# Token tiles of 504 and 496 columns in place of 512 and 384

## The chip, the cores and the metric

The kernel runs on one core of one Trainium2 chip. The metric is the device time of one execution in microseconds. Engines are named as the profile names them: PE is TensorE's matmul, PEld its weight load, DVE is VectorE, ACT is ScalarE, POOL is GpSimd, SP is SyncE, whose queue issues nearly all DMAs.

## The reference, cut to what matters

```python
def _attn_ref(q, k, v, tau):                 # B, N, C = 2, 6016, 256
    qn = q / (np.linalg.norm(q, axis=1, keepdims=True) + 1e-06)
    kn = k / (np.linalg.norm(k, axis=1, keepdims=True) + 1e-06)
    s = kn.transpose(0, 2, 1) @ qn / tau     # 256 x 256 for each batch
    a = softmax(s)
    return v @ a                             # 6016 tokens x 256

def _moe_ref(x, w_gate, w_val, w_out):       # d_ff 1536
    gate = 1.0 / (1.0 + np.exp(-(x @ w_gate)))
    return gate * (x @ w_val) @ w_out

def _moe2_ref(x, w_in, w_out):               # d_ff 2048
    h = x @ w_in
    return (h - np.tanh(h)) @ w_out

x = attn(q, k, v, tau).reshape(12032, 256)
out = _moe2_ref(_moe_ref(x))
```

The attention is over channels: scores are 256 x 256 for each batch, and the softmaxed matrix multiplies every token of the batch. What follows works on each token by itself. So 12032 tokens, 6016 in each of two batches, run through four products, and how they are cut into tiles is free, but that a tile may not reach over the end of a batch.

## The kernel before

The kernel holds tokens as columns. A tile is a range of at most 512 tokens of one batch, since 512 float32 numbers fill one bank of PSUM. `token_tiles` (lines 57 to 66) makes the list: eleven tiles of 512 and one of 384 in the first batch, and the same turned round in the second, so that the two tiles of 384 are neighbours, the 12th and the 13th of 24.

Before the tiles run, about the first 57 us, the scores of the first batch are summed over 47 groups of 128 token rows (`qk_scores`, L278), normalized and softmaxed, and the attention matrix is multiplied into the gate and value weights (`aw_block`). With that the value product of the attention disappears as a step of its own: stage 1 multiplies the raw v by those combined weights.

Data for the matmuls are split into a high and a low part of type float32r, so each product takes three matmuls: weight high by data high, weight low by data high (`prod_h`, L475 and L476), weight high by data low (`prod_l`, L480). For each tile i:

- Stage 1, 12 units c: `s1_mm` makes the gate and value products of 128 hidden channels each, two PSUM tiles `ps` with six matmuls each. ACT takes the sigmoid (L515), DVE multiplies (L516). `part_b` splits the result (L580 on ACT, L581 on DVE or GpSimd), and `part_c` adds it into two accumulators `y` (six matmuls).
- Stage 2, 16 units m: `s2_mm` makes `h` (six matmuls), `s2_a` works out h - tanh(h) on ACT and DVE (L539 to L560), `part_b` splits, `part_c` adds into two accumulators `o` (six matmuls). After the last unit they are copied out and sent (L642, L643).

So a tile takes 12 x 12 + 12 x 6 + 16 x 6 + 16 x 6 = 408 matmuls, each over all columns of the tile. The order of the work is written out: a list of units is sorted by a position that goes by the unit's number alone, not by its columns, and stage 2 of a tile runs between the units of stage 1 of the next. Each unit's three parts follow each other with a lag of three units. In between, from the third tile on, a list of side steps makes the scores of the second batch (matmuls of 256 columns, L283 to L285) and then its combined weights.

PSUM has eight banks. Four of them are a ring, from which `ps`, `h` and the side steps' tiles are taken. A new tile in the ring waits, on TensorE, until the last reader of the tile that had its bank is done. The program hands out the banks when it is built, and not strictly in turn.

v is loaded a tile ahead (`load_v`, L339): the load for tile i + 1 is issued when tile i has been split. The very last unit works on two halves of its tile (`HALVES`, L585, and `finish`), so that the two halves overlap on the way out.

Of the kernel before, what the change touches and what calls it, by code (L numbers as in the profile page):

```python
# [18 lines left out]
B, S, D = 2, 6016, 256  # L19
# [4 lines left out]
TPB = 12  # L24
CH = 512
NM = 512
NW = 12
NO = 6
NI = 8
# [27 lines left out]
def token_tiles():  # L57
    out = []
    for b in range(B):
        off = 0  # L60
        sizes = [NM] * (S // NM) + [S % NM]
        for n in sizes if b < B - 1 else sizes[::-1]:
            out.append((b, off, b * S + off, n))
            off += n
        assert off == S
    return out
# [3 lines left out]
def attn_moe_kernel(  # L70
# [125 lines left out]
    wo_t = [base.tile([P, 2, CH], F32R, name=f"wo{c}") for c in range(NO)]  # L196
    wgv_d = dram.tile([NW // 2, P, 2, 2, CH], F32, name="wgv_d")


    wgv_t = [wp.tile([P, 2, 2, CH], F32R, name=f"wgv{f}") for f in range(NW // 2)]  # L200

    def wgv_item(f, jc):
        return (wgv[2 * f + jc], lambda: wgv_t[f][:, :, jc, :], f"wgv{f}_{jc}")

    def wo_item(c):
        return (wo[c], lambda: wo_t[c], f"wo{c}")

    conv0 = [wgv_item(0, jc) for jc in range(2)]
    conv = [wgv_item(1, jc) for jc in range(2)]
    for f in range(2, NW // 2):  # L210
        conv += [wgv_item(f, 0), wgv_item(f, 1), wo_item(f - 2)]
# [107 lines left out]
    def aw_block(aT, rs, wt, ic, dst, name):  # L319
# [8 lines left out]
        nc.vector.scalar_tensor_tensor(dst[:, 1, ic, :], ps, rs[:, ic : ic + 1], dst[:, 0, ic, :].bitcast(F32), op0=ALU.mult, op1=ALU.subtract)  # L328

    tiles = token_tiles()  # L330
    NT = len(tiles)
    raws, vhl = {}, {}

    def load_v(i):
        if i >= NT:
            return
        b, off, _, n = tiles[i]
        t = vp.tile([P, 2, NM], F32, tag="vraw", name=f"vraw{i}")
        nc.sync.dma_start(t[:, :, :n], vT[b].rearrange("(c p) n -> p c n", p=P)[:, :, off : off + n])  # L339
        raws[i] = t  # L340

    def split_v(i, between=lambda: None, eng=nc.vector):
        n = tiles[i][3]
        t = raws.pop(i)
        vhl[i] = [vp.tile([P, 2, NM], F32R, tag=f"vhl{ic}", name=f"vhl{i}_{ic}") for ic in range(2)]
        for ic in range(2):
# [61 lines left out]
    for t in (1, 0):  # L408
        for c in range(2):
            o = 2 * (2 * t + c)  # L410
# [37 lines left out]
    def new_aw(f, b):  # L448
        return ap_.tile([P, 2, 2, CH], F32R, tag=f"aw{f}", name=f"aw{f}_{b}")

    aws = {0: [new_aw(f, 0) for f in range(NW // 2)], 1: []}
    mp = ctx.enter_context(tc.tile_pool(name="mp", bufs=1, reuse_waits="tile"))
    aT0 = mp.tile([P, 2, 2, D], F32R, name="aT0", tag="yhl")
    for ic in range(2):
        cs = slice(ic * P, (ic + 1) * P)
# [17 lines left out]
    def prod_h(ps, n, wts, xs, first, skip=False):  # L473
        for j, ((wh, wl), (xh, _)) in enumerate(zip(wts, xs)):
            mm(ps[:, :n], wh, xh, start=first and j == 0, stop=False, skip_group_check=skip)  # L475
            mm(ps[:, :n], wl, xh, start=False, stop=False, skip_group_check=skip)  # L476

    def prod_l(ps, n, wts, xs, last, skip=False):
        for j, ((wh, _), (_, xl)) in enumerate(zip(wts, xs)):
            mm(ps[:, :n], wh, xl, start=False, stop=last and j == len(wts) - 1, skip_group_check=skip)  # L480
# [30 lines left out]
    def s1_act(i, c):  # L511
        n = tiles[i][3]
        G, V = live[1, i, c]
        sg = mp.tile([P, NM], F32, tag="sg", bufs=2, name=f"sg{i}_{c}")
        nc.scalar.activation(sg[:, :n], G[:, :n], AF.Sigmoid)  # L515
# [13 lines left out]
    def late(i, m):  # L529
        return i == NT - 2 and m >= LATE or i == NT - 1 and m < K2 - 1  # L530

    def s2_a(i, m, mid):
        n = tiles[i][3]
        H = live[2, i, m][:, :n]
        u = m2.tile([P, NM], F32, tag="u", bufs=2, name=f"u{i}_{m}")[:, :n]
        d = m2.tile([P, NM], F32, tag="d", bufs=2, name=f"d{i}_{m}")[:, :n]
        s = (yp if m % 2 and (i == NT - 1 or late(i, m)) else m2).tile([P, NM], F32, tag="s", bufs=2, name=f"s{i}_{m}")[:, :n]
# [11 lines left out]
        else:  # L549
# [5 lines left out]
            else:  # L555
                mid()
                nc.scalar.activation(big, u, AF.Relu, bias=c_m[:, 0:1])
            for cs in HALVES if (2, i, m) == LAST else (slice(0, n),):
                nc.vector.scalar_tensor_tensor(s[:, cs], s[:, cs], C_D, w[:, cs], op0=ALU.add, op1=ALU.mult)
# [13 lines left out]
    def part_b(u):  # L573
# [4 lines left out]
        eng = nc.gpsimd if kind == 2 and (late(i, c) or u[1:] == LAST or c < 2 * i < 6) else nc.vector  # L578
        for cs in HALVES if u[1:] == LAST else (slice(0, n),):
            nc.scalar.copy(hl[:, 0, cs], x[:, cs])  # L580
            (nc.vector if cs == HALVES[1] else eng).tensor_sub(hl[:, 1, cs], x[:, cs], hl[:, 0, cs].bitcast(F32))  # L581
        live[kind, i, c] = hl

    LAST = (2, NT - 1, K2 - 1)
    HALVES = [slice(h * NM // 2, (h + 1) * NM // 2) for h in range(2)]  # L585

    def finish(hl, ws, pos):

        acc = ops[NT - 1]

        def high(o, h):
            prod_h(acc[o][:, HALVES[h]], NM // 2, [ws[o]], [(hl[:, 0, HALVES[h]], None)], False, True)

        def low(o, h):
            prod_l(acc[o][:, HALVES[h]], NM // 2, [ws[o]], [(None, hl[:, 1, HALVES[h]])], True, True)

        def put(o):
            for h, cs in enumerate(HALVES if o else [slice(0, NM)]):
                t = m2.tile([P, NM], F32, tag=("out", "d")[h], bufs=2, name=f"out{NT - 1}_{o}_{h}")
                (nc.scalar.copy if o else nc.vector.tensor_copy)(t[:, cs], acc[o][:, cs])  # L600
                (nc.scalar if h else nc.sync).dma_start(outT[o * P : (o + 1) * P, pos + cs.start : pos + cs.stop], t[:, cs])

        high(0, 0)
        high(1, 0)
        high(0, 1)
        low(0, 0)
        low(0, 1)
        put(0)
        high(1, 1)
        low(1, 0)  # L610
        low(1, 1)
        put(1)
# [122 lines left out]
    def wblock(f):  # L735
        if f < NW // 2:
            t = qp.tile([P, 2, 2, CH], F32R, tag="wb", name=f"wb{f}")
            nc.sync.dma_start(t.bitcast(F32), wgv_d[f])
            q1["wb", f] = t

    def side_aw(f, ic):
# [4 lines left out]
        if ic == 1:  # L746
            wblock(f + 1)
            if f + 1 == NW // 2:
                q2ctx.close()
# [164 lines left out]
```

## Time and profile before

| what | value |
|---|---|
| time, median of 3 runs | 2304.48 us (2304.45 to 2304.77) |
| the profiled execution | 2304.04 us |
| its span, first to last instruction | 2302.2 us |
| PE busy | 2296.7 us, 10434 matmuls recorded |
| PEld busy | 1928.0 us |
| DVE busy | 1815.5 us |
| ACT busy | 1582.1 us |
| POOL busy | 83.1 us |
| mean granted clock of TensorE | 0.999 of 2.4 GHz |
| DMA | 83.08 MB, mean 36 GB/s |

The span is what the profile sees; the 1.8 us between it and the execution's time lie before its first and after its last instruction. An engine's busy time says in how much of the span it had something under way. For a pipelined engine like TensorE that can be all of the span although it works below its pace; its pace is read from the starts of its instructions.

### The profile page before, as it was taken

What the parts mean: (1) busy time and instruction counts of PE and PEld (TensorE: products, weight loads), DVE (VectorE), ACT (ScalarE), POOL (GpSimd) and SP (SyncE); (2) the same over time, 40 slices, a digit from 0 to 9 for tenths busy, and PEclk for the clock granted to TensorE, in tenths of its full rate; (3) what the DMA queues carried; (4) which work ended last, traced back from release to release, by engine and by line L of the source; (5) the groups of instructions that cost most, each with busy time, mean ns of one, the idle gap of its engine ahead of it and who ended that gap; (6) DMA issues with size and microseconds to landing.
All of it is one profiled execution on the core that took longest, in us unless ns stands there. A gap on an engine that the chain in (4) does not pass through costs nothing.

```text
span 2302.2 us, 28360 instructions
## 1 busy us (share of the span) xinstructions
PE 2296.7 (100%) x10434; PEld 1928.0 (84%) x10434; DVE 1815.5 (79%) x2891; ACT 1582.1 (69%) x2884; POOL 83.1 (4%) x64
## 2 busy tenths in 40 slices
PE   9999999999999999999999999999999999999999
PEld 8888888888888888888899988888888888888887
DVE  6878879888888888877777777777777777786778
ACT  7657777676776677766666666666666667666668
POOL 5000000000000000000000000000000000000007
PEclk9999999999999999999999999999999999999999
DMA  8630001110101101001110000000000000000000
GB/s 333 248 114 1 24 23 33 33 37 19 37 28 33 37 23 37 4 32 35 55 37 17 6 11 19 1 19 10 10 19 2 18 19 1 19 10 10 10 1 19
DMA packets 39786, 83.08 MB, mean 36 GB/s; under 512 B 4192, under 2 KB 18272, under 8 KB 38112
## 3 DMA queue, kind: packets, MB, share of 16 engines
q1 hardware_dynamic: 39216, 80.89, 10.4%
q8 instruction: 81, 1.33, 0.2%
q14 instruction: 57, 0.47, 0.1%
q10 hardware_dynamic: 432, 0.39, 0.1%
HBM read 62.39 MB, written 18.87 MB: 35 GB/s over the span
## 4 chain that ended last, share of the span: by engine, by line
PE 99%; ACT 0%; DMA 0%; issue 0%; POOL 0%; SPq 0%
PE ps L476 11%; PE ps L475 11%; PE ps L480 11%; PE o L480 7%; PE h L476 7%; PE h L480 7%; PE h L475 7%; PE o L475 7%; PE o L476 7%; PE y L480 6%; PE y L476 6%; PE y L475 6%; PE S0o L278 1%; PE S0y L278 1%; PE aw L326 0%; PE aw L325 0%
## 5 line engine op out<-in xcount | busy, mean ns | idle before, releaser
L476 PE MATMUL ps<-vhl,aw 128*128 128x512 f32 (+1 forms) x1152 | 443.6, 385 | 0.0
L475 PE MATMUL ps<-vhl,aw 128*128 128x512 f32 (+1 forms) x1152 | 443.5, 385 | 0.0
L544 DVE TENSOR_TENSOR d<-h,d 128x512 f32<-128x512 f32 (+1 forms) x366 | 247.8, 677 | 237.1 <-ACT d L540 237.0
L580 ACT CAST hl<-s 128x512 fp32r<-128x512 f32 (+1 forms) x385 | 235.2, 611 | 274.8 <-DVE s L548 271.9
L539 ACT ACTIVATE u<-h 128x512 f32<-128x512 f32 (+1 forms) x384 | 226.7, 590 | 242.5 <-PE h L480 242.0
L480 PE MATMUL ps<-vhl,aw 128*128 128x512 f32 (+1 forms) x1152 | 349.8, 385 | 0.0
L546 DVE TENSOR_TENSOR u<-h,u 128x512 f32<-128x512 f32 (+1 forms) x360 | 243.3, 676 | 108.6 <-ACT big L543 108.5
L475 PE MATMUL o<-hl,wv 128*128 128x512 f32 (+2 forms) x770 | 295.8, 384 | 0.0
L476 PE MATMUL o<-hl,wv 128*128 128x512 f32 (+2 forms) x770 | 295.8, 384 | 0.0
L476 PE MATMUL h<-yhl,wi 128*128 128x512 f32 (+1 forms) x768 | 295.7, 385 | 0.0
L475 PE MATMUL h<-yhl,wi 128*128 128x512 f32 (+1 forms) x768 | 295.6, 385 | 0.0
L548 DVE COPY_PREDICATED s<-big,d 128x512 f32<-128x512 int16 (+1 forms) x366 | 269.8, 737 | 12.9
L541 ACT ACTIVATE s<-u,c_b 128x512 f32<-128x512 f32 (+1 forms) x384 | 276.1, 719 | 2.0 <-DVE hl L581 2.0
L543 ACT ACTIVATE big<-u,c_m 128x512 bf16<-128x512 f32 (+1 forms) x366 | 260.4, 712 | 0.0
L547 DVE SCALAR_TENSOR_TENSOR s<-s,u 128x512 f32<-128x512 f32 (+1 forms) x360 | 246.0, 683 | 12.7
L475 PEld LDWEIGHTS ps<-vhl,aw 128*128 128x128 f32 x1152 | 216.4, 188 | 40.9 <-ACT sg L515 0.3
L476 PEld LDWEIGHTS ps<-vhl,aw 128*128 128x128 f32 x1152 | 216.3, 188 | 40.7
L480 PEld LDWEIGHTS ps<-vhl,aw 128*128 128x128 f32 x1152 | 215.6, 188 | 41.5
L516 DVE TENSOR_TENSOR sg<-ps,sg 128x512 f32<-128x512 f32 (+1 forms) x288 | 194.1, 674 | 67.2 <-PE ps L480 49.9
L581 DVE TENSOR_TENSOR hl<-s,hl 128x512 fp32r<-128x512 f32 (+2 forms) x355 | 236.9, 667 | 0.6 <-ACT hl L580 0.5
L480 PE MATMUL o<-hl,wv 128*128 128x512 f32 (+2 forms) x770 | 234.2, 385 | 0.2 <-POOL hl L581 0.2
L515 ACT ACTIVATE sg<-ps 128x512 f32<-128x512 f32 (+1 forms) x288 | 170.1, 591 | 92.6 <-PE ps L480 87.0
(170 smaller groups left out, 3601.7 us busy)
## 6 DMA issues: line engine op xcount, KB each, us to landing
vraw<-in_vT_dram SPq DMA_DIRECT2D x22, 512.0 KB, 3.7
out_dram<-out SPq DMA_DIRECT2D x43, 256.0 KB, 2.2
raw_wgv<-in_wgv_dram SPq DMA_DIRECT2D x12, 512.0 KB, 4.6
wgv_d<-wgv SPq DMA_DIRECT2D x6, 1024.0 KB, 11.7
wb<-wgv_d SPq DMA_DIRECT2D x6, 1024.0 KB, 4.8
raw<-in_q_dram SPq DMA_DIRECT2D x47, 128.0 KB, 2.1
raw<-in_k_dram SPq DMA_DIRECT2D x47, 128.0 KB, 2.2
rawq<-in_q_dram SPq DMA_DIRECT2D x8, 512.0 KB, 9.9
```

What stands on the lines that cost most here:

```text
L475: mm(ps[:, :n], wh, xh, start=first and j == 0, stop=False, skip_group_check=skip)
L476: mm(ps[:, :n], wl, xh, start=False, stop=False, skip_group_check=skip)
L480: mm(ps[:, :n], wh, xl, start=False, stop=last and j == len(wts) - 1, skip_group_check=skip)
L539: nc.scalar.activation(u, H, AF.Square)
L541: nc.scalar.activation(s, u, AF.Square, scale=C_S, bias=c_b[:, 0:1])
L543: nc.scalar.activation(big, u, AF.Relu, bias=c_m[:, 0:1])
L544: nc.vector.tensor_sub(d, H, d)
L546: nc.vector.tensor_mul(w, H, u)
L547: nc.vector.scalar_tensor_tensor(s, s, C_D, w, op0=ALU.add, op1=ALU.mult)
L548: nc.vector.copy_predicated(s, big.bitcast(I16), d)
L580: nc.scalar.copy(hl[:, 0, cs], x[:, cs])
L581: (nc.vector if cs == HALVES[1] else eng).tensor_sub(hl[:, 1, cs], x[:, cs], hl[:, 0, cs].bitcast(F32))
```

## The change

The list of sizes becomes a constant: each batch is cut into eight tiles of 504 and four of 496 tokens, in the second batch four of 496 and eight of 504. There are still 24 tiles, 12 in a batch, and 8 x 504 + 4 x 496 = 6016. The buffers in SBUF and PSUM keep their 512 columns (`NM`). The last tile now has 504 columns, so its halves, which were cut by `NM`, are cut by its own width into 252 and 252.

```diff
+WIDTHS = [504] * 8 + [496] * 4
@@ token_tiles
-        sizes = [NM] * (S // NM) + [S % NM]
-        for n in sizes if b < B - 1 else sizes[::-1]:
+        for n in WIDTHS if b < B - 1 else WIDTHS[::-1]:
             out.append((b, off, b * S + off, n))
@@
-    HALVES = [slice(h * NM // 2, (h + 1) * NM // 2) for h in range(2)]
+    NL = tiles[-1][3]
+    HALVES = [slice(h * NL // 2, (h + 1) * NL // 2) for h in range(2)]
@@ finish
-            prod_h(acc[o][:, HALVES[h]], NM // 2, [ws[o]], [(hl[:, 0, HALVES[h]], None)], False, True)
+            prod_h(acc[o][:, HALVES[h]], NL // 2, [ws[o]], [(hl[:, 0, HALVES[h]], None)], False, True)
...
-            for h, cs in enumerate(HALVES if o else [slice(0, NM)]):
+            for h, cs in enumerate(HALVES if o else [slice(0, NL)]):
```

The instructions stand in the same order on all five engines, in the same number; their widths differ, and some waits.

On TensorE, in stage 1 of the 13th tile, the gate and value products of its second unit (`ps_1_0`, `ps_1_1`), then the 15th addition into the 11th tile's accumulators (`o_0`, `o_1`). Before:

```order
L480 MATMUL ps_1_0_10751<-vhl_1_10622,aw_1_9898 128x384
L475 MATMUL ps_1_1_10752<-vhl_0_10621,aw_1_9898 128x384 [waits Activation_49]
L476 MATMUL ps_1_1_10752<-vhl_0_10621,aw_1_9898 128x384
L475 MATMUL ps_1_1_10752<-vhl_1_10622,aw_1_9898 128x384
L476 MATMUL ps_1_1_10752<-vhl_1_10622,aw_1_9898 128x384
L480 MATMUL ps_1_1_10752<-vhl_0_10621,aw_1_9898 128x384
L480 MATMUL ps_1_1_10752<-vhl_1_10622,aw_1_9898 128x384
L475 MATMUL o_0_10035<-hl_10_14_10698,wv_998 128x512
```

And of the changed kernel, the same place:

```order
L480 MATMUL ps_1_0_10751<-vhl_1_10622,aw_1_9898 128x496
L475 MATMUL ps_1_1_10752<-vhl_0_10621,aw_1_9898 128x496 [waits DVE_49]
L476 MATMUL ps_1_1_10752<-vhl_0_10621,aw_1_9898 128x496
L475 MATMUL ps_1_1_10752<-vhl_1_10622,aw_1_9898 128x496
L476 MATMUL ps_1_1_10752<-vhl_1_10622,aw_1_9898 128x496
L480 MATMUL ps_1_1_10752<-vhl_0_10621,aw_1_9898 128x496
L480 MATMUL ps_1_1_10752<-vhl_1_10622,aw_1_9898 128x496
L475 MATMUL o_0_10035<-hl_10_14_10698,wv_998 128x496 [waits Activation_49]
```

The value product's bank was last read by ACT before and is now one that DVE read last, a combined-weight tile of the second batch; the wait on ACT moves to the first `o` matmul. All of these now have 496 columns.

On TensorE, the end of the program, the last unit with its two halves. Before:

```order
L475 MATMUL o_0_20229<-hl_23_15_20587,wv_998 128x256 [waits Activation_49]
L476 MATMUL o_0_20229<-hl_23_15_20587,wv_998 128x256
L475 MATMUL o_1_20230<-hl_23_15_20587,wv_998 128x256
L476 MATMUL o_1_20230<-hl_23_15_20587,wv_998 128x256
L475 MATMUL o_0_20229<-hl_23_15_20587,wv_998 128x256 [waits Activation_49]
L476 MATMUL o_0_20229<-hl_23_15_20587,wv_998 128x256
L480 MATMUL o_0_20229<-hl_23_15_20587,wv_998 128x256 [waits Pool_49]
L480 MATMUL o_0_20229<-hl_23_15_20587,wv_998 128x256 [waits DVE_49]
```

And of the changed kernel:

```order
L475 MATMUL o_0_20229<-hl_23_15_20587,wv_998 128x252 [waits Activation_49]
L476 MATMUL o_0_20229<-hl_23_15_20587,wv_998 128x252
L475 MATMUL o_1_20230<-hl_23_15_20587,wv_998 128x252
L476 MATMUL o_1_20230<-hl_23_15_20587,wv_998 128x252
L475 MATMUL o_0_20229<-hl_23_15_20587,wv_998 128x252 [waits Activation_49]
L476 MATMUL o_0_20229<-hl_23_15_20587,wv_998 128x252
L480 MATMUL o_0_20229<-hl_23_15_20587,wv_998 128x252 [waits Pool_49]
L480 MATMUL o_0_20229<-hl_23_15_20587,wv_998 128x252 [waits DVE_49]
```

Nothing moves here; the halves have 252 columns, the only matmuls of the split data below 256.

## Rows read from the trace of the kernel before

**Rows 1.** The page: TensorE's busy time, and its granted clock in 40 slices.

```profile
PE 2296.7 (100%) x10434; PEld 1928.0 (84%) x10434; DVE 1815.5 (79%) x2891; ACT 1582.1 (69%) x2884; POOL 83.1 (4%) x64
...
PEclk9999999999999999999999999999999999999999
```

**Rows 2.** The page: the chain that ended last, shares by engine.

```profile
PE 99%; ACT 0%; DMA 0%; issue 0%; POOL 0%; SPq 0%
```

**Rows 3.** Busy time by stretch, PE alone (stretch, its length, busy, count, clock, DMA).

```profile
1185.00:1240.00 55.00, 55.00 (x319) 1.00 0.00 1
...
1400.00:2200.00 800.00, 800.00 (x3531) 1.00 0.04 12
```

**Rows 4.** Timeline of PE (start us, length us): widths 256, 512, 384.

```profile
600.44 0.28 PE L283 MATMUL qk<-hl 128*128 128x256 f32 x1
...
601.15 0.40 PE L475 MATMUL h<-yhl,wi 128*128 128x512 f32 x1
...
603.90 0.39 PE L475 MATMUL ps<-vhl,aw 128*128 128x512 f32 x1
...
605.26 0.39 PE L475 MATMUL ps<-vhl,aw 128*128 128x512 f32 x1
...
1124.04 0.33 PE L475 MATMUL ps<-vhl,aw 128*128 128x384 f32 x1
...
1125.10 0.33 PE L475 MATMUL ps<-vhl,aw 128*128 128x384 f32 x1
...
1126.14 0.33 PE L475 MATMUL y<-hl,wo 128*128 128x384 f32 x1
...
1127.18 0.39 PE L475 MATMUL h<-yhl,wi 128*128 128x512 f32 x1
```

**Rows 5.** Busy time by stretch: first 60 us, and first to last 384-wide matmul (columns: PE, PEld, DVE, ACT, POOL).

```profile
0.00:60.00 60.00, 58.79 (x262) 49.45 (x263) 38.18 (x76) 44.63 (x77) 29.21 (x25) 1.00 0.86 322
...
1071.42:1336.05 264.63, 264.63 (x1351) 242.37 (x1350) 198.59 (x351) 175.93 (x353) 0.00 (x0) 1.00 0.10 32
```

**Rows 6.** Groups of L541 by shape (mean ns), and busy time by stretch.

```profile
L541 ACT ACTIVATE s<-u,c_b 128x512 f32<-128x512 f32 x352 | 256.3, 728 | 2.0 <-DVE hl L581 2.0
...
L541 ACT ACTIVATE s<-u,c_b 128x384 f32<-128x384 f32 x32 | 19.9, 620 | 0.0
...
1200.00:1250.00 50.00, 50.00 (x281) 48.84 (x280) 40.58 (x79) 34.68 (x76) 0.00 (x0) 1.00 0.04 11
...
2200.00:2250.00 50.00, 50.00 (x222) 41.41 (x221) 35.72 (x55) 34.77 (x64) 8.82 (x7) 1.00 0.00 1
```

**Rows 7.** Timeline: a bank's last reader, and the first matmul of `ps_1_1`.

```profile
1172.52 0.75 DVE L328 SCALAR_TENSOR_TENSOR aw<-aw,rs,aw 128x512 fp32r<-128x512 f32 x1
...
1174.21 0.33 PE L475 MATMUL ps<-vhl,aw 128*128 128x384 f32 x1
```

**Rows 8.** DMA issues (KB, us to landing); landing times of L601, then L643.

```profile
vraw<-in_vT_dram SPq DMA_DIRECT2D x22, 512.0 KB, 3.7
...
DMA to landing us min/median/max: 2.0/2.1/2.4
...
DMA to landing us min/median/max: 1.9/2.2/3.9
```

**Rows 9.** Timeline of the tail, with what ended an idle time.

```profile
2294.30 1.30 POOL L581 TENSOR_TENSOR hl<-s,hl 128x512 fp32r<-128x512 f32 x1 [0.92 <-POOL hl L581]
...
2295.65 0.73 PE L480 MATMUL o<-hl,wv 128*128 128x512 f32 x2 [0.24 <-POOL hl L581]
...
2296.20 0.74 POOL L581 TENSOR_TENSOR hl<-s,hl 128x256 fp32r<-128x256 f32 x1 [0.60 <-ACT hl L580]
```

**Rows 10.** Timeline of PE: score products of the first batch, unsplit float32 data.

```profile
38.34 3.62 PE L278 MATMUL S0o<-rawq,rawk 128*128 128x256 f32 x16
41.79 0.50 PE L411 MATMUL nps<-const-float32-1.0,sumk 128*128 128x2 f32 x4
```

More of the change, by code (lines that the diff above doesn't have):

```diff
@@ L591, in high @@
         def high(o, h):
-            prod_h(acc[o][:, HALVES[h]], NM // 2, [ws[o]], [(hl[:, 0, HALVES[h]], None)], False, True)
+            prod_h(acc[o][:, HALVES[h]], NL // 2, [ws[o]], [(hl[:, 0, HALVES[h]], None)], False, True)
         def low(o, h):
-            prod_l(acc[o][:, HALVES[h]], NM // 2, [ws[o]], [(None, hl[:, 1, HALVES[h]])], True, True)
+            prod_l(acc[o][:, HALVES[h]], NL // 2, [ws[o]], [(None, hl[:, 1, HALVES[h]])], True, True)
         def put(o):
-            for h, cs in enumerate(HALVES if o else [slice(0, NM)]):
+            for h, cs in enumerate(HALVES if o else [slice(0, NL)]):
                 t = m2.tile([P, NM], F32, tag=("out", "d")[h], bufs=2, name=f"out{NT - 1}_{o}_{h}")
```

## The prediction

> **What bounds the kernel now.** I read the page's first two parts, then the chain that ended last, then TensorE's own rows. TensorE is busy for 2296.7 of 2302.2 us, and the clock row stands at its upper level, 2.4 GHz, from start to end [rows 1]. The chain that set the end is 99% TensorE [rows 2]. A busy engine is not yet one at its limit, so the next thing to see is the distance from the start of one matmul to the start of the next. The means of 385 to 390 ns in the groups of the page are no help: they run from a matmul's start to its modelled end, and neighbours overlap. Starts are what counts.
>
> Between 1400 and 2200 us, where all tiles are 512 wide, 3531 matmuls are under way, one or two of them only at an edge: 800 us by 3529 to 3530 is 226.6 to 226.7 ns each [rows 3]. Inside the 384-wide stretch it is 55 us by 317 to 318, 173.0 to 173.5 ns [rows 3]. Six starts in a row say the same: 1.36 us at 512 columns, 1.04 us at 384, 0.71 us at 256 (the second batch's score products), so 227, 173 and 119 ns [rows 4]. At 2.4 GHz, 512, 384 and 256 columns alone take 213.3, 160.0 and 106.7 ns. The remainder is 13.3 ns at the first two widths and 12 to 13 at the third. So one matmul costs **(columns + 32) / 2.4 ns**, a straight line through three widths. Put against all start times, the sum of matmuls at this price is the elapsed time to within 0.3 us in every 50 us, but for the first 100 us, 900 to 1000, the mixed stretch below and the tail. Elsewhere TensorE waits for nothing that narrower tiles could deliver earlier.
>
> **The change, part by part.**
>
> *Columns and instructions of the tile work.* A tile needs 12 x 12 matmuls for the gate and value products, 12 x 6 for the first output, 16 x 6 and 16 x 6 for the second layer: 408. There were 24 tiles and there are 24. Before: 22 x 408 x 226.67 + 2 x 408 x 173.33 ns = 2034.6 + 141.4 = 2176.0 us. After, by the line: 504 columns cost 223.33 ns and 496 cost 220.00 ns, so 16 x 408 x 223.33 + 8 x 408 x 220.00 = 1457.9 + 718.1 = 2176.0 us. The columns sum to 12032 either way and the 32 are paid equally often. **Zero**, as long as the line holds between its points; that is the assumption on which the forecast stands, and the first two rivals attack it.
>
> *The mixed stretch.* Where 384- and 512-wide matmuls alternate, the spacing leaves the line a little. From the first 384-wide matmul, at 1071.42 us, to the end of the last, at 1336.05 us, 816 of 384 and 534 of 512 columns start. At the line they take 141.4 + 121.0 = 262.5 us, the stretch takes 264.6 [rows 5]: 2.1 us more. It is seen in the rows: six 384-wide matmuls just after a 512-wide one take 1.06 us, six in the midst of their kind 1.04 [rows 4]. After, there are again two mixed stretches (504 beside 496, at the eighth and at the sixteenth tile), but the neighbours differ by 8 columns in place of 128. No row shows what that costs. Bounds: all of it stays, 0, or all goes, -2.1; I take the middle, **-1.1 us**.
>
> *ACT and DVE.* Each instruction per tile becomes cheaper or dearer by its columns: the square of L541 takes 728 ns at 512 and 620 at 384 [rows 6], 0.84 ns a column, so about 721 at 504. The instructions are as many as before, so their sum is the same too. What hides it is TensorE's own work: in a pure 512 stretch DVE is busy 35.7 of 50 us and ACT 34.8, in the pure 384 stretch 40.6 and 34.7 [rows 6]. At 504 and 496 the shares lie between these, and TensorE stalled in neither. **Zero.**
>
> *Which PSUM bank.* The four banks of the ring are not handed out in strict turn, and with other widths the program hands them out differently from the sixth tile on, so some waits move to other matmuls. Comparing whose reader must have finished before which first matmul, I find 14 places where the reader is another one. The tightest is the value product of the second unit of the 13th tile: it now waits for the DVE eviction of an aw block, which ended at 1172.52 + 0.75 = 1173.27 us; the matmul starts at 1174.21 [rows 7]. 0.94 us to spare there, over 2 us at all others. What is queued behind such a matmul is the whole of TensorE's work, so a shortfall would count in full; with these margins it is **zero**.
>
> *DMA.* Loads of v shrink from 512 KB to about 500 and land in 3.7 us [rows 8]; each is issued a tile ahead, some 90 us of TensorE work. Outputs but the last leave beside later tiles. Zero.
>
> *The tail.* The last tile goes from 512 to 504 columns and its halves from 256 to 252. On GpSimd, 1.30 us at 512 and 0.74 at 256 [rows 9] give 2.2 ns a column, 17 ns for eight; the VectorE and ScalarE steps of the last chain give some 8 ns each at about 1 ns a column. TensorE's second waiting matmul pair (2295.65, held 0.24 us by GpSimd) follows them. Estimate **-0.05 us**. Two prices are unknown there. First, 252 is below every width that the split data has had in this trace; twelve matmuls have it. By the line each saves 1.7 ns. The dear end is the price of an unsplit product of 256 columns: sixteen matmuls in 41.79 - 38.34 = 3.45 us [rows 10], 216 ns, and two per product. Twelve at 431 in place of 120 ns is +3.7 us. I take the line, from the nearest row, 256 columns at 119 to 120 ns of the same kind of data. Second, the last two transfers now begin 32 bytes past a 256-byte boundary instead of on one. They landed within 2.4 us, and the slowest output of the run took 3.9 against a median of 2.2 [rows 8], so 0 to +1.7 us; I take **+0.1**, since outputs of half the size land in nearly the same time. The Trainium skill, "DMA: Bandwidth & Descriptors", section "How a descriptor splits into AXI transactions", has a rule that speaks against the new offsets: a descriptor that starts off such a boundary is served from the boundary below it, so a row of 1008 bytes would need five transactions where 1024 aligned ones needed four. An estimate from that page is a quarter more on the transfer's own part of those 2 us, under +0.3 us, and the sum would be 2303.7 in place of 2303.5; no run here shows it yet.
>
> *Sum.* 0 - 1.1 - 0.05 + 0.1 = -1.05 us. On the profiled execution that is 2304.04 - 1.05 = 2303.0 us (the span 2301.2, with 1.8 us around it as before). The median of the runs stands 0.44 us higher than this execution, so 2303.5 us. With the bounds, -2.2 and +5.4 (3.7 + 1.7), this case runs from 2302.2 to 2309.9; the upper end needs both unlucky prices at once.
>
> **The rivals.**
>
> *A coarser step (slower).* If TensorE takes columns in steps of 16, 504 costs as much as 512 while 496 keeps its price: 16 x 408 x 3.33 ns = +21.8 us, 2326 us. If the step is 32 or more, both cost as 512: 8 x 408 x 6.67 ns more, +43.5 us, 2348 us. The place is every matmul of the 24 tiles, and it decides from a step of 16 on. For it: every width in this trace is a multiple of 128, so no row excludes it. Against it: nothing in the rows has a step at all. Chance 0.08.
>
> *The 32 columns are a rounding (faster).* A small fixed part rounded up to the next multiple of 32 would give columns + 32 at 256, 384 and 512, too; then 504 and 496 would both end at 512 columns, 213.3 ns. That saves 16 x 408 x 10.0 + 8 x 408 x 6.67 ns = 87 us, 2217 us. For it: it fits all three points. Against it: the unsplit 256-column matmuls, two columns' time per column, are spaced by 215.6 ns [rows 10], 517 columns' time, which is no multiple of 32. Chance 0.04.
>
> *Out of step (slower).* The disturbed spacing of the mixed stretch, 20 ns in six or 3.3 ns a matmul [rows 4], could be the normal state of widths that are no multiple of 128: 9792 x 3.3 ns = +32 us, 2337 us. Against it: six 256-wide matmuls amid 512-wide ones are not dearer [rows 4]. Chance 0.03.
>
> *The change does not do what it says.* Order and number of the instructions are the same on all five engines, with 504, 496 and 252 where 512, 384 and 256 stood; nothing is left for this but 0.02, to either side.
>
> **How the numbers follow.** About 0.2%, 4.6 us, is what a measurement of this kernel can tell from no change: 2299.9 to 2309.1. The forecast has 0.83, of which 0.81 lies within; 0.01 goes to either side for the tail's and the start's prices. Faster: 0.04 + 0.01 + 0.01 = 0.06. Slower: 0.08 + 0.03 + 0.01 + 0.01 = 0.13. The range, 2300.5 to 2309.0, holds the forecast's case but for its farthest corner, and leaves the rivals out.
>
> **What would show it.** Right: starts in a pure 504 stretch 223.3 ns apart and in a pure 496 stretch 220.0; TensorE busy over all of the span; the stretches around the eighth and sixteenth tiles within 2 us of the line; the last twelve matmuls no dearer than 120 ns; the last output landing within 2.5 us. Wrong: 226.7 ns at 504 (a step), 213.3 (a rounding), about 226.6 (out of step, told from a step by 496, which would cost near 223), or idle time of TensorE before a gate product, which would mean a bank came free too late. The first 60 us, which hold the scores of the first batch [rows 5], should not move.

## The result and the profile after

| | before | after |
|---|---|---|
| median | 2304.45 us (2304.34 to 2304.77) | 2326.38 us (2325.85 to 2326.42) |
| span of the profiled execution | 2302.2 us | 2324.6 us |
| PE busy | 2296.7 us | 2319.4 us |

The ratio is 1.0095, 95% interval 1.008 to 1.0109: **slower by 0.95%**, about 22 us, where no change was forecast. The page of the changed kernel, engine busy times, the granted clock in 40 slices, and the chain that ended last by engine:

```profile
PE 2319.4 (100%) x10434; PEld 1941.7 (84%) x10434; DVE 1815.7 (78%) x2891; ACT 1585.4 (68%) x2884; POOL 82.3 (4%) x64
...
PEclk9999999999999999999999999999999999999999
...
PE 99%; ACT 0%; issue 0%; POOL 0%
```

Beside [rows 1] and [rows 2]: the same number of matmuls, the same clock, still TensorE alone on the chain, DVE and ACT as busy as before to within 3.3 us. So nothing new is waited for; TensorE's own work has become 22.7 us longer. The busy time by stretch (PE alone: stretch, its length, busy time and matmuls, granted clock, DMA share, GB/s) answers to [rows 3]:

```profile
100.00:300.00 200.00, 200.00 (x884) 1.00 0.18 60
960.00:1050.00 90.00, 90.00 (x407) 1.00 0.07 24
1200.00:1500.00 300.00, 300.00 (x1365) 1.00 0.03 11
1700.00:2200.00 500.00, 500.00 (x2208) 1.00 0.04 12
```

The stretch from 100 to 300 us was pure 512 before:

```profile
100.00:300.00 200.00, 200.00 (x884) 1.00 0.17 57
```

One or two matmuls of each count are only under way at an edge. The first and the last row after the change are pure 504: 884 matmuls in 200 us, the same count as with 512 columns before, and 500 us by 2206 to 2207 is **226.6 ns**, the price of 512 columns. The line said 223.3. The second and third row are 496 wide, but for four 128-wide matmuls (109 ns each) in the second, and they differ: 90 us by 405 to 406 is 222 ns with those four (from the starts, the 496s alone are 223.3 apart on average for most of the stretch, a little more where the second batch's norms come in), and 300 us by 1363 to 1364 is 220.0, the line. **One width, two prices, within one execution.** The place where one goes over into the other is in the timeline of PE (start us, length us, instruction). The row of 1079.15 is the first of six 512-wide matmuls of a combined-weight block:

```profile
1077.81 0.39 PE L475 MATMUL o<-hl,wv 128*128 128x496 f32 x1
1078.03 0.39 PE L476 MATMUL o<-hl,wv 128*128 128x496 f32 x1
1078.26 0.39 PE L475 MATMUL o<-hl,wv 128*128 128x496 f32 x1
...
1079.15 0.39 PE L324 MATMUL aw<-wb,aT 128*128 128x512 f32 x1
...
1080.54 0.39 PE L475 MATMUL h<-yhl,wi 128*128 128x496 f32 x1
1080.76 0.38 PE L476 MATMUL h<-yhl,wi 128*128 128x496 f32 x1
1080.98 0.38 PE L475 MATMUL h<-yhl,wi 128*128 128x496 f32 x1
1081.20 0.38 PE L476 MATMUL h<-yhl,wi 128*128 128x496 f32 x1
...
1081.86 0.38 PE L475 MATMUL y<-hl,wo 128*128 128x496 f32 x1
```

Ahead of the block six 496-wide matmuls take 1079.15 - 1077.81 = 1.34 us, behind it 1081.86 - 1080.54 = 1.32; in the full start times a mean of 223.3 ns turns into 220 each. From there on the 496s stay at 220 until 1532 us, where 504s come between them and they go back to 223.3.

Where the 22.4 us of span went, from the start times of all matmuls, as time over the line (columns + 32) / 2.4 ns between the first 60 us and the tail:

| matmuls | before | after |
|---|---|---|
| 512 columns | 9052, +4.2 us | 120, +0.1 us |
| 384 | 816, +0.8 us | none |
| 504 | none | 6483, **+22.3 us** |
| 496 | none | 3264, **+4.5 us** |
| 256 | 260, -0.1 us | 260, +0.1 us |
| sum | 4.9 us | 27.0 us |

That is +22.1 us. The first 60 us give +0.4, the tail -0.3, and the copy and the output behind the last matmul +0.2: 22.4 in all.

### The profile page after: what moved, and what is told of

Same layout as the page of the kernel before. It is cut to its first block, busy times and chain, and to the rows that moved or that the text cites. A ratio compares the mean times of both kernels' runs of the same rounds, so it can differ in the third digit from the quotient of the medians.

```text
span 2324.6 us, 28360 instructions
## 1 busy us (share of the span) xinstructions
PE 2319.4 (100%) x10434; PEld 1941.7 (84%) x10434; DVE 1815.7 (78%) x2891; ACT 1585.4 (68%) x2884; POOL 82.3 (4%) x64
## 4 chain that ended last, share of the span: by engine, by line
PE 99%; ACT 0%; issue 0%; POOL 0%
PE ps L475 11%; PE ps L476 11%; PE ps L480 11%; PE h L476 7%; PE h L480 7%; PE h L475 7%; PE o L480 7%; PE o L476 7%; PE o L475 7%; PE y L476 6%; PE y L480 6%; PE y L475 6%; PE S0o L278 1%; PE S0y L278 1%; PE aw L326 0%; PE aw L324 0%
## 5 line engine op out<-in xcount | busy, mean ns | idle before, releaser
L475 PE MATMUL ps<-vhl,aw 128*128 128x504 f32 (+1 forms) x1152 | 446.1, 387 | 0.0
L476 PE MATMUL ps<-vhl,aw 128*128 128x504 f32 (+1 forms) x1152 | 445.9, 387 | 0.0
L544 DVE TENSOR_TENSOR d<-h,d 128x504 f32<-128x504 f32 (+1 forms) x366 | 248.2, 678 | 253.1 <-ACT d L540 252.6
L480 PE MATMUL ps<-vhl,aw 128*128 128x504 f32 (+1 forms) x1152 | 352.6, 387 | 0.0
L546 DVE TENSOR_TENSOR u<-h,u 128x504 f32<-128x504 f32 (+1 forms) x360 | 243.8, 677 | 110.5 <-ACT big L543 110.2
L475 PE MATMUL o<-hl,wv 128*128 128x504 f32 (+2 forms) x770 | 297.6, 387 | 0.0
L476 PE MATMUL o<-hl,wv 128*128 128x504 f32 (+2 forms) x770 | 297.6, 387 | 0.0
L475 PE MATMUL h<-yhl,wi 128*128 128x504 f32 (+1 forms) x768 | 297.4, 387 | 0.0
L476 PE MATMUL h<-yhl,wi 128*128 128x504 f32 (+1 forms) x768 | 297.2, 387 | 0.0
L548 DVE COPY_PREDICATED s<-big,d 128x504 f32<-128x504 int16 (+1 forms) x366 | 270.3, 739 | 13.1
L541 ACT ACTIVATE s<-u,c_b 128x504 f32<-128x504 f32 (+1 forms) x384 | 275.7, 718 | 1.9 <-DVE hl L581 1.9
L543 ACT ACTIVATE big<-u,c_m 128x504 bf16<-128x504 f32 (+1 forms) x366 | 260.9, 713 | 0.0
L547 DVE SCALAR_TENSOR_TENSOR s<-s,u 128x504 f32<-128x504 f32 (+1 forms) x360 | 245.9, 683 | 12.8
L581 DVE TENSOR_TENSOR hl<-s,hl 128x504 fp32r<-128x504 f32 (+2 forms) x355 | 237.0, 668 | 0.6 <-ACT hl L580 0.5
L480 PE MATMUL o<-hl,wv 128*128 128x504 f32 (+2 forms) x770 | 235.7, 387 | 0.1
```

Of the source, the lines that this page charges most:

```text
L541: nc.scalar.activation(s, u, AF.Square, scale=C_S, bias=c_b[:, 0:1])
L544: nc.vector.tensor_sub(d, H, d)
L546: nc.vector.tensor_mul(w, H, u)
L547: nc.vector.scalar_tensor_tensor(s, s, C_D, w, op0=ALU.add, op1=ALU.mult)
L548: nc.vector.copy_predicated(s, big.bitcast(I16), d)
```

## Experiments

Three questions: is 504 charged by a step in the columns (the rival "coarser step", which had 2326 us)? Is it the neighbours (the rival "out of step")? And does the price hang on where data, weights or results lie? The expectations below call the theories by letters: A is the step of 16 columns, B the out-of-step theory, C a fixed fee for widths that are no multiple of 16, D a step of 8; F, formed after the first runs, is a rhythm that the stream of matmuls falls into and keeps, G that what ran before plays no part. Each kernel is the changed one but for the list of widths, if nothing else is said. The stretches named are pure ones, in which only the width in question runs.

**Widths 512 and 496.**

```diff
-WIDTHS = [504] * 8 + [496] * 4
+WIDTHS = [512] * 4 + [496] * 8
```

> Each batch in four tiles of 512 and eight of 496, all widths multiples of 16, otherwise the changed kernel. Theory A (TensorE takes columns in steps of 16): 496 costs 220.0 ns and 512 costs 226.7 ns, the tile work is 2176.0 us as before the change, so 2303 to 2306 us. Theory B (tiles of nearly equal width, or widths that are no multiple of 128, cost by being out of step): the loss stays, 2320 us or more. Theory C (a fee of 8 columns' time for any width that is no multiple of 16): as A.

Measured 2309.5 us (ratio to before 1.0022, 1.0013 to 1.0031). Neither A's 2303 to 2306 nor B's 2320. Busy time by stretch, pure 496 in both:

```profile
1000.00:1050.00 50.00, 50.00 (x226) 1.00 0.00 1
1200.00:1800.00 600.00, 600.00 (x2729) 1.00 0.04 12
```

About 224 and 2727 to 2728 starts: 223.3 and 220.0 ns. In the first batch all 496s between 500 and 1050 us go at the dear price, in the second all at the cheap one. So with 504 gone most of the loss is gone, and what is left, 8.8 us over the line on 6528 matmuls of 496, is the same two prices as after the change. A step cannot do that.

**Widths 508 and 500.**

```diff
-WIDTHS = [504] * 8 + [496] * 4
+WIDTHS = [508] * 2 + [500] * 10
```

> Each batch in two tiles of 508 and ten of 500, no width a multiple of 8. Theory A (steps of 16): both cost as 512, 226.7 ns, 9792 x 226.67 = 2219.5 us of tile work, 43.5 more than before: 2347 to 2350 us. Theory C (a fee of 8 columns for any width that is no multiple of 16): every matmul 3.33 ns above the line, 228.3 and 225.0 ns, +32.6 us: about 2337 us. Theory D (steps of 8, with something else at 504): 508 as 512 and 500 as 504 by the line, 226.7 and 223.3 ns, about 2315 us plus what that is.

Measured 2322.5 us (1.0077, 1.0063 to 1.0091), in none of the three places. Busy time by stretch, the first two pure 500 but for four 128-wide matmuls in the first, the third pure 508:

```profile
960.00:1050.00 90.00, 90.00 (x400) 1.00 0.07 24
1250.00:2000.00 750.00, 750.00 (x3360) 1.00 0.04 12
...
2200.00:2250.00 50.00, 50.00 (x221) 1.00 0.00 0
```

500 columns go at about 226 ns in the one stretch (226.7 from most of its starts) and at 223.3 in the other, 508 at 227.6, more than 512. **Theory A falls**: 500 lies between 496 and 512 and mostly costs 223.3, less than 504 does. C and D fall with it, since a fee or a smaller step would give one price per width.

**The price of a width by itself.** A kernel of its own: a stream of 72 matmuls of each width, three times this loop, with only an addition on DVE behind each.

```python
for i in range(24):
    a = (i % 4) * 128
    nc.tensor.matmul(ps[:, po : po + n], w[:, a : a + 128], x[:, off : off + n], start=i == 0, stop=i == 23)
```

> Computes none of the reference: only streams of 72 matmuls of one width after another, on TensorE alone, to measure the price of a width by itself; its time is not to be compared. Split-type data (float32r) at widths 512, 510, 508, ... 480, 384, 376, 256, 252, 248, 240; then moving data that start 4 or 8 columns into their row, results that start 8 columns into their bank; then bfloat16 and unsplit float32. Theory A (steps of 16 columns): 498 to 510 at 226.7 ns, 484 to 496 at 220.0, 480 at 213.3, 376 at 173.3, 252 and 248 at 120.0, 240 at 113.3. Theory C (a fee of 8 columns): 510 at 229.2, 500 at 225.0, 492 at 221.7, 252 at 121.7. If the step counts 64-byte pieces of the row that are touched, 496 columns that begin 8 columns in touch 32 pieces and cost 226.7; if it counts columns, they cost 220.0. bfloat16 at 504 and 496 tells whether a step is 16 columns or 64 bytes (32 columns of that type: 496 would cost as 512).

Here and in the two streams below, the spacing is worked out from the start times of each piece's later part. Float32r: 226.7 ns at 512, 510, 506, 504, 500 and 498; 227.6 at 508; 223.3 at 502 and 496; 222.2 at 492; 225.6 at 488, 218.7 at 484, 216.7 at 480; 173.3 at 384 and at 376 alike; 120.0 at 256, 116.7 at 252, 115.0 at 248, 111.9 at 240. No step gives this list: it isn't even rising, 488 costs more than 492. Moving data or results that begin 4 or 8 columns in changed 504 not at all (226.7) and 496 by at most 1.1 ns (223.3 to 224.4). **The other data types have none of it** at the widths tried: bfloat16 at 512, 504, 500, 496: 215.8, 212.5, 210.8, 209.2 ns, which is (columns + 6) / 2.4; unsplit float32, where each matmul leaves two records, at 256, 252, 248: 215.8, 212.5, 209.2 for each record, which is (2 x columns + 6) / 2.4. Two stretches of bfloat16 (512, then 504) and two of unsplit float32 (256, then 252):

```profile
377.00:390.00 13.00, 13.00 (x62) 1.00 0.00 0
393.00:405.00 12.00, 12.00 (x58) 1.00 0.00 0
...
440.00:466.00 26.00, 26.00 (x122) 1.00 0.00 1
470.00:497.00 27.00, 27.00 (x128) 1.00 0.00 1
```

The Trainium skill, "TensorE: Matmul & The Clock Gate", section "Back-to-back issue gap", gives columns / 2.4 + 2.5 ns as the isolated gap of a single matmul at the upper clock, and about 131 ns at 512 columns for a stream of weight loads and matmuls. The rows of bfloat16, a stream with a weight load for each matmul, agree with the first (215.8 against 215.8 ns at 512) and not with the second; the float32r rows agree with neither (226.7). The measurement decides.

**Eight columns for nothing.** 15 of the 16 tiles of 504 are computed 512 wide.

```diff
-            out.append((b, off, b * S + off, n))
+            out.append((b, off, b * S + off, 512 if n == 504 and off + 512 <= S else n))
...
-                    nc.sync.dma_start(outT[o * P : (o + 1) * P, pos : pos + n], t[:, :n])
+                    no = (tiles[i + 1][2] if i + 1 < NT else B * S) - pos
+                    nc.sync.dma_start(outT[o * P : (o + 1) * P, pos : pos + no], t[:, :no])
```

> The changed kernel, but 15 of its 16 tiles of 504 tokens (all but the very last) are computed 512 columns wide: the eight columns more are the next tile's first tokens, worked out twice and not written out here. If 504 columns cost TensorE what 512 do (226.7 ns, as the changed kernel's trace shows), nothing is added: 2325 to 2328 us. If columns were paid by the line, 15 x 408 x 3.33 ns = 20.4 us are added: 2347 us.

Measured 2326.8 us (1.0098, 1.0084 to 1.0112), beside 2326.4 for the changed kernel: 120 columns more per product, 1% of all columns, cost nothing that can be measured. In this kernel eight columns of 512 are free because 504 had already paid for them.

**One batch alone.** First batch as before the change, second as after it.

```diff
-        for n in WIDTHS if b < B - 1 else WIDTHS[::-1]:
+        for n in [512] * 11 + [384] if b < B - 1 else WIDTHS[::-1]:
```

> First batch cut as before the change (eleven of 512, one of 384), second as after it (four of 496, eight of 504). The price is put on the 504-wide matmuls alone: 8 x 408 x 3.33 ns = 10.9 us over the kernel before, less up to 2 us of the mixed stretch: 2313 to 2316 us. If the loss came from the cut as a whole, or from the first batch's side work: 2304 or 2326 us.

Measured 2319.1 us (1.0064, 1.0048 to 1.0079), 3 us above the expectation. From the starts: 504 gives +11.2 us, as expected, and the four tiles of 496, which follow the 384s here, all go at 223.3: +5.4 us. A stretch of pure 496:

```profile
1300.00:1500.00 200.00, 200.00 (x897) 1.00 0.03 11
```

In the changed kernel about nine tenths of the 496s behind the first combined-weight block (1986 of the 2196 between 1079 and 1637 us) went at 220. This points to what stands ahead of the 496s, and not to which tile they are. That is theory F, and the next two runs test it in the whole kernel.

**496 behind 384, and behind 512.** Two kernels with the same first batch as before and the same widths in the second; one tile of 512 changes its place.

```diff
-        for n in WIDTHS if b < B - 1 else WIDTHS[::-1]:
+        for n in [512] * 11 + [384] if b < B - 1 else [496] * 8 + [512] * 4:
```

```diff
-        for n in WIDTHS if b < B - 1 else WIDTHS[::-1]:
+        for n in [512] * 11 + [384] if b < B - 1 else [512] + [496] * 8 + [512] * 3:
```

> First batch as before the change, second in eight tiles of 496 and four of 512. Theory F (split-type matmuls keep one of a few rhythms; 496 has two, 220.0 and 223.3 ns, and which one it falls into is set by what ran before): behind the 512-wide combined-weight matmuls of the 12th tile it falls into 220.0, as in the second batch of the run with 512 and 496: 2303 to 2305 us. If it falls into 223.3: 8 x 408 x 3.33 = +10.9, 2315 us. Theory A (steps of 16 columns) has 220.0 always, so 2303 to 2305 us.

> First batch as before the change (eleven of 512, one of 384); second in one tile of 512, eight of 496, three of 512: against the run with eight of 496 and then four of 512 behind the 384, only one tile of 512 is moved ahead of the 496s. Theory F (a run of 512 columns puts the 496s into their cheap rhythm, a run of 384 into the dear one, and it is kept): 496 at 220.0 ns, 8 x 408 x 3.33 = 10.9 us less at most than the run it is compared with, so 2303 to 2306 us. Theory G (the neighbours have no part): 496 at 223.3 as there, 2313 us.

The one took 2313.4 us (1.004, 1.0027 to 1.0052), against my expectation of 2303 to 2305: the 512-wide combined-weight blocks did not set the cheap price here, where they run amid 384s; no run shows how many of them would have been needed. The other took **2304.3 us** (1.0000, 0.9991 to 1.0009). The same stretch of each, pure 496 in both, first the one, then the other:

```profile
1400.00:1800.00 400.00, 400.00 (x1793) 1.00 0.04 12
```

```profile
1400.00:1800.00 400.00, 400.00 (x1820) 1.00 0.04 12
```

400 us by 1791 to 1792 is 223.3 ns, by 1818 to 1819 it is 220.0. Moving one tile of 512 ahead of eight tiles of 496 is worth 9.1 us, at the same columns, instructions and amount of data. This is the plainest evidence for F.

**The rhythm by itself.** The same loop ten times for each width, with a choice of neighbours; first with `w[:, a : a + wc]` for weights of `wc` columns, then with short runs of other widths between.

> Computes none of the reference: streams of 240 matmuls of split-type data of one width after another, on TensorE alone; its time is not to be compared. Theory F: 496 and perhaps 504 take different spacings behind 512, 504, 384 and 256. Theory A: one spacing each, 220.0 and 226.7. Further, weights of 64 and of 32 columns in place of 128: if the 32 columns on top of each matmul are the time in which its weights are fetched, 512 columns go from 226.7 to 220.0 and 216.7 ns, and the widths that are no multiple of 128 come nearer to the line; if they are not, 226.7 stays.

496 columns behind 512, 504, 384 and 256, then 504 columns behind 512, 384 and 256, and last 512 columns with weights of 64:

```profile
65.00:115.00 50.00, 50.00 (x229) 1.00 0.00 1
228.00:278.00 50.00, 50.00 (x225) 1.00 0.00 0
322.00:372.00 50.00, 50.00 (x226) 1.00 0.00 1
405.00:455.00 50.00, 50.00 (x226) 1.00 0.00 1
...
173.00:223.00 50.00, 50.00 (x222) 1.00 0.00 0
500.00:550.00 50.00, 50.00 (x222) 1.00 0.00 0
583.00:633.00 50.00, 50.00 (x222) 1.00 0.00 1
...
976.00:1026.00 50.00, 50.00 (x219) 1.00 0.00 0
```

504 columns go at 226.7 ns behind 512, behind 384 and behind 256. 496 go at 220.0 behind 512 and at 223.3 behind 504, 384 and 256. Each keeps its mean over its 240 but for the first few. **Singly the dear spacings are not equal**: behind 384 the 496s repeat 223, 227, 222 and 221 ns over and over, and 500 columns take 221 and 226 by turns, while the cheap 496s take 220 each. Further: 500 at 223.3, 488 at 220.0, 480 at 216.7, 448 at 202.7, 416 at 188.3, and 400 at 180.0, 384 at 173.3, on the line. With weights of 64 columns in place of 128, 512 go at 230.0 and with 32 at 231.7: not 220.0 and 216.7. So the 32 columns on top of each matmul are not the fetching of so many weight columns. The weights' width does change the other prices: 504 and 496 go at 230.6 and 225.0 with 64 columns, and at 226.7 and 220.0 with 32. So behind 504s the 496s took 220.0 with 32 weight columns and 223.3 with 128.

> Computes none of the reference: streams of 240 matmuls of split-type data on TensorE alone, with a few matmuls of another width between them; its time is not to be compared. Theory F (a rhythm that is kept until something disturbs it): 496 columns go at 220.0 ns behind 512, are thrown to 223.3 by a few matmuls of 256, 384 or 504 columns, and come back to 220.0 behind one to 24 of 512. Theory G (what ran just before does not matter; the state is set by something else, such as where the data lie): the same spacing in all of them, or changes that go with no neighbour. 504 columns with one and the same weights, with moving data that shift by 16 columns, and with results that alternate between two banks: 226.7 ns in all if neither weights, data nor banks have a part in it; 223.3, the line, in the one that has.

Between pieces of 240 at 496 columns, in this order, a few others: behind 240 of 512, 220.0; then six of 256, 223.3; six of 512, 220.0; six of 384, 223.3; one of 512, 223.3; six of 504, 223.3; twenty-four of 512, 220.0; two of 256, 223.3; two of 512, 223.3. The first four pieces, by stretch:

```profile
66.00:116.00 50.00, 50.00 (x229) 1.00 0.00 1
120.00:170.00 50.00, 50.00 (x226) 1.00 0.00 1
176.00:226.00 50.00, 50.00 (x230) 1.00 0.00 1
230.00:280.00 50.00, 50.00 (x226) 1.00 0.00 0
```

A count of 229 or 230 in 50 us is 220 ns, of 226 it is 223.3. Six matmuls of 512 set the cheap rhythm, one or two are not enough, and two of 256 are enough to lose it; each was tried once. The six of 504 came when the price was dear already, so that 504s undo the cheap one is shown by the 240 of them above and by the changed kernel from 1532 us on. 504 with one and the same weights, with shifting moving data and with results alternating between two banks: 226.7 each time; 496 behind 512 with one weight or with two banks: 220.0. So a change of weights and the banks have no part in these prices, and where the data begin has none in that of 504. Six of 512 don't do the same for every width: 500 went at 223.3 behind one such run and at 226.7 behind another.

**A cut made for the rhythm.**

```diff
-        for n in WIDTHS if b < B - 1 else WIDTHS[::-1]:
+        for n in [512, 400] + [512] * 9 + [496] if b < B - 1 else [496] * 8 + [512] * 4:
```

> A cut made for the rhythm: first batch one of 512, one of 400, nine of 512, one of 496, second eight of 496 and four of 512, so that the 496s begin behind 512 and after the 256-wide side products are through. 400 went at its line price in the stream by itself. Theory F: all tiles at the line but for the mixed stretches around the tile of 400, no mixed stretch in the middle: 2302 to 2305 us, at best 2 us under the kernel before. Theory G: eight or nine tiles of 496 at 223.3: 2313 us or more.

Measured 2305.1 us (1.0004, 0.9995 to 1.0012), at the upper end of what I expected and not below the kernel before. A stretch of pure 496, and the one in which the tile of 400 begins:

```profile
1200.00:1800.00 600.00, 600.00 (x2729) 1.00 0.04 12
100.00:150.00 50.00, 48.96 (x249) 1.00 0.56 192
```

In the second batch all 496s go at 220.0, and the stretch in which 496 and 512 mix has no time over the line, where the 384s of before cost 2.1 us. The tile of 400 costs more than that: 3.3 us between 100 and 350 us, 1.2 of it TensorE idle, which has no gap there with the cut of before. No cut that was tried beats the one of before.

## Why the prediction was wrong

*What bounds the kernel*: right. TensorE alone, at a granted clock of 2.4 GHz, before and after.

*Columns and instructions*: **the step that failed.** The sum 2176.0 us rested on a straight line through 256, 384 and 512 columns. At 504 the price was 226.67 ns in place of 223.33, +22.3 us on 6483 matmuls, and at 496 partly 223.33 in place of 220.00, +4.5 us. Why the engine takes that long at 504 stays open; 504 was never seen on the line. The three widths of [rows 4] lie on the line exactly, and no row of before held another width in any number; three points on a line did not say that the points between lie on it. The text named this as its assumption and gave the three rivals against it 0.15.

*The mixed stretch*: the direction was right and the row held more than was read from it. The six 384-wide matmuls behind 512 that take 1.06 us [rows 4] start 171, 175, 177, 185, 176 and 182 ns apart, and the six 384s behind 496s in the last stream above, where TensorE waits for no other engine, repeat these six spacings to the nanosecond. So the time over the line there belongs to TensorE itself. I read it as the price of unlike neighbours and expected less of it from like ones. After, the 384s and nearly all 512s, with their 5.0 us over the line, are gone, but the 496s that begin among 504s keep the dear price, from 950 to 1079 us even by themselves: +4.5.

*The coarser step*: its time, 2326 us, is the measured one, and its mechanism is not what happened. 504 does cost as 512 does and 496 can cost 220.0, which is all that a step of 16 says of this kernel; but 500 at 223.3, 488 at 220.0 and at 225.6, and 496 at two prices have no step. The sum agrees by luck: the 4.5 us lost at 496 nearly equal the 5 us that went with the old cut.

*Out of step*: the nearest to what the runs show, given 0.03. Its size, 3.3 ns a matmul, is what the dear rhythm adds at 496 and what 504 pays above the line, though with weights of 128 columns no run shows 504 at a second price. It went wrong in taking this for all matmuls (+32 us): 1986 of the 3264 496s kept the cheap rhythm, and 400, no multiple of 128 either, went on the line in a stream by itself. The argument against it, six 256s amid 512s that are not dearer, was about the wrong widths: 512 and 256 are back on the line after a few matmuls, 496 stays off it.

*The rounding*: did not happen; 504 and 496 never went below means of 226.7 and 220.0 ns, where it wanted 213.3, and no width of the split data lay under the line by more than 1.7 ns.

*ACT, DVE, the ring's banks, DMA*: right at zero. In the changed kernel a pure 504 stretch has DVE busy for 35.6 and ACT for 32.0 of 50 us, and TensorE without a gap:

```profile
2200.00:2250.00 50.00, 50.00 (x222) 41.44 (x221) 35.56 (x56) 32.04 (x59) 1.27 (x1) 1.00 0.00 1
```

Nor has TensorE a gap anywhere else between 60 and 2310 us. The bank that had 0.94 us to spare was free 2.15 us ahead of its matmul (1172.55 and 1174.70 us).

*The tail*: right. The rows that answer to [rows 9], and the landing of the last outputs:

```profile
2318.03 0.72 PE L480 MATMUL o<-hl,wv 128*128 128x504 f32 x2
2318.46 0.73 POOL L581 TENSOR_TENSOR hl<-s,hl 128x252 fp32r<-128x252 f32 x1 [0.49 <-ACT hl L580]
2318.59 0.28 PE L475 MATMUL o<-hl,wv 128*128 128x252 f32 x1
...
2318.94 0.28 PE L476 MATMUL o<-hl,wv 128*128 128x252 f32 x1
...
DMA to landing us min/median/max: 2.0/2.2/2.5
```

Three spacings at 252 columns in 0.35 us: no dearer than at 256, so the +3.7 us bound was empty. The outputs land in at most 2.5 us against 2.4, the last matmul's start is 4.5 us ahead of the end against 4.3: too little to tell from nothing. One reading was wrong: of the last two transfers only the first begins 32 bytes past a 256-byte boundary, the second, at token 11780 with 4 bytes each, begins 16 past one. The first landed in 2.5 us (2.1 before), the second in 2.2 (2.4 before). The Trainium skill, "DMA: Bandwidth & Descriptors", section "How a descriptor splits into AXI transactions", has the first transaction of a descriptor that does not start on such a boundary start at the boundary below it; the estimate that the prediction drew from it, under 0.3 us more, is not contradicted by these rows and not shown by them.

## What to carry to other kernels

A price that is linear at the widths that a trace holds need not be so between them: before a kernel that TensorE bounds is cut into other widths, run a stream of just those widths, in their type, and behind the neighbours that they will have. With split float32r data keep to the widths that were on the line here (512, 384 and 256), and if a narrower one must be used, look for its spacing twice, behind unlike and behind like neighbours. A model whose sum comes out right can still have the wrong reason; a width or two outside the pair at hand told them apart.

## What was not expected of the hardware

At some widths float32r matmuls run in one of two or more steady rhythms, which are kept for hundreds of microseconds and whose mean spacings differ: 496 columns at 220.0 or 223.3 ns, 500 at 223.3 or 226.7, 488 at 220.0 or 225.6. Six matmuls of 512 columns set the lower one for 496; two of 256, six of 384 or a stretch of 504 undo it. Bfloat16 keeps to (columns + 6) / 2.4 ns and unsplit float32 to (2 x columns + 6) / 2.4 for each record, in the same stream. What in the engine makes this rhythm is open: one weight or several and the banks made no difference to it, the place of the data at most 1.1 ns. Narrower weights shifted the prices (512 from 226.7 to 230.0 and 231.7 ns), so a part of the weight loads, which run beside every matmul, is neither shown nor excluded.
